# Joint attention block: transposes sorted by width, three value groups of six accumulators, gate rows beside the text scores, gate folded into the last output columns

## The chip, the cores and the metric

The kernel runs on one core of one Trainium2 chip. The core has a matrix engine (TensorE, PE in the profile, with its weight loads as a row of their own, PEld), VectorE (DVE), ScalarE (ACT), GpSimd (POOL) and SyncE (SP), which issues most DMAs. The metric is device time of one execution in microseconds (us). The kernel before takes 124.08 us, median of three runs (123.66 to 124.31).

## The reference

Image tokens (2 batches of 256) and text tokens (2 batches of 32), all of width 1152, are normalised, scaled and shifted by rows computed from a conditioning vector, projected to queries, keys and values with separate weights, attended jointly, projected out with separate weights, gated and added to the input:

```python
hi = _layernorm(x_img) * (1 + sci) + shi      # text: ht, with sct and sht
qkvi = hi @ wqkv_img                          # text: qkvt = ht @ wqkv_txt
q = jnp.concatenate([qt, qi], axis=1)         # k and v likewise: 288 tokens a batch
scores = jnp.einsum('bqd,bkd->bqk', q, k) * D ** (-0.5)
p = _softmax(scores, axis=-1)
a = jnp.einsum('bqk,bkd->bqd', p, v)
out_i = x_img + gai * (ai @ wo_img)
out_t = x_txt + gat * (at @ wo_txt)
```

gai and gat are the third of six slices of silu(c) @ wmod; only the first three slices are used. All is bfloat16 in memory, sums are float32.

## The kernel before, in words

The order of every engine's work is written by hand; a tile framework adds the semaphores. Fourteen weight blocks of 1152 x 1152 (2.6 MB each) are loaded by SyncE's queue into six buffers that are used in turn (`wpool`). PSUM, where matmuls write, is held as seven banks in turn (`ps_mm`) and one more (`ps_sm`).

Up to about 78 us the kernel normalises and projects. Then come the stages that the change touches.

- Scores. `scores_txt` (L456) computes the 32 text queries of both batches, the two batches side by side in tiles of 128 rows by 32 columns. `scores_img(b, qi)` (L448) computes 128 image queries against the batch's 288 keys with 9 matmuls. Each is followed by a softmax: a maximum on VectorE, an exponential with row sum on ScalarE. The text weights are divided by their sum at once (`softmax_txt_norm`); the image rows are divided only at the output. `mod_rows(w_ga_i, 3)` (L344) computes the image gate row for both batches in four tiles of 128 x 32; it goes through a scratch in device memory (L354) and comes back, broadcast to all partitions, as `gb` (L543), both by POOL's queue. The order is: text scores, two image blocks of batch 0, gate rows, two image blocks of batch 1.
- Transposes. `p_transposes(b)` turns the softmax weights with TensorE: for each image block two 128 x 128 pieces (L486, image keys) and two copies of the 32 text keys, at the partitions where text values will lie (L488, 128*32), then the text queries' pieces (L493, 32*128, and L496, 32*32). ScalarE copies the image-key part out of PSUM as `pT` (L499), VectorE the text-key part as `pX` (L501). `v_txt` computes the text values between the two batches' transposes: 1024 columns in two tiles side by side (L525), then the remaining 128 (L528).
- Value stage. `attn_out` makes the attention output transposed, in nine tiles of 128 columns for each batch: `aT`. Groups of two column tiles and two batches, four accumulators, and a last group of two: first the image keys (L510, 128*128, two matmuls each), then the text keys (L516, 32*128, one each; the four of a group lie in four different row strips). The casts to `aT` alternate between VectorE and ScalarE (`evac`, L142 and L144).
- Output. `out_tile(i)` (L578) multiplies 128 image tokens with the output weights, in chunks of 384 columns and nine matmuls; VectorE multiplies a chunk with the inverse row sum and the gate (L581) and adds the input (L583), and SP's queue stores it. The order is image tiles 0 and 1, the text gate rows, image tile 2, the text output (L597, L601, L602, stored by SP and by ScalarE's queue, L605), and image tile 3 in chunks of 384, 384, 256 and 128 with a store for each (L585).

Of the kernel before, what the change touches and what calls it, by code (L numbers as in the profile page):

```python
# [9 lines left out]
ALU = mybir.AluOpType  # L10
# [4 lines left out]
def kernel(  # L15
# [14 lines left out]
    nc = tc.nc  # L30
    bf = mybir.dt.bfloat16
    f32 = mybir.dt.float32
    PSUM = bass.MemoryType.PSUM

    B, NI, D = x_img.shape
    NT = x_txt.shape[1]
    P = 128
    KT = D // P
    NTOK = NI + NT
    NIT = (B * NI) // P  # L40
    TPB = NI // P
    NTT = B * NT
    CH = 384
# [10 lines left out]
    wpool = ctx.enter_context(tc.tile_pool(name="w", bufs=6))  # L54
    act = ctx.enter_context(tc.tile_pool(name="act", bufs=1))
    work = ctx.enter_context(tc.tile_pool(name="work", bufs=2))
    small = ctx.enter_context(tc.tile_pool(name="small", bufs=4))
    ps_mm = ctx.enter_context(tc.tile_pool(name="ps_mm", bufs=7, space=PSUM))
    ps_sm = ctx.enter_context(tc.tile_pool(name="ps_sm", bufs=1, space=PSUM))
# [22 lines left out]
    x_i = act.tile([P, NIT, D], bf)  # L82
# [25 lines left out]
    ident = const.tile([P, P], bf)  # L108
# [186 lines left out]
    v_t = act.tile([P, VW], bf)  # L295
    v_t8 = act.tile([NTT, P], bf)
    pbs = {}
# [13 lines left out]
    ps = ps_mm.tile([P, VW], f32, tag="mm")  # L311
# [24 lines left out]
    NGG = 4  # L336
    gsc = tc.dram_tile([5, B, D], bf, name="mod_scratch")

    def mod_rows(w_blk, si, add_one=False, lhs=None):
        lhs = sT32 if lhs is None else lhs  # L340
        gps = ps_mm.tile([P, VC], f32, tag="mm")
        for kt in range(KT):
            for g in range(NGG):
                nc.tensor.matmul(gps[32 * g:32 * g + 32, :], lhsT=lhs[:, kt, :], rhs=w_blk[:, kt, g * VC:(g + 1) * VC],  # L344
                                 start=(kt == 0), stop=(kt == KT - 1), tile_position=(0, 32 * g))
        g_sb = work.tile([P, VC], bf, tag="garow")
        if add_one:
            nc.vector.tensor_scalar_add(g_sb[:], gps[:], 1.0)
        else:
            evac(g_sb[:], gps[:])  # L350
        if si is None:
            return g_sb
        for b in range(B):
            nc.gpsimd.dma_start(gsc[si, b, :].rearrange("(g j) -> g j", g=NGG), g_sb[b:P:32, :])  # L354
# [89 lines left out]
    def scores_img(b, qi):  # L444
        q0 = qi * P
        sps = ps_mm.tile([P, NTOK], f32, tag="mm")
        for ft in range(KT):
            nc.tensor.matmul(sps[:], lhsT=qkT[:, ft, b, q0:q0 + P], rhs=qkT[:, KT + ft, b, :],  # L448
                             start=(ft == 0), stop=(ft == KT - 1))
        softmax_img(sps, (b, qi))  # L450

    def scores_txt():
        sps = ps_mm.tile([P, NTOK], f32, tag="mm")
        for ft in range(KT):
            for b in range(B):
                nc.tensor.matmul(sps[NT * b:NT * (b + 1), :], lhsT=qkT[:, ft, b, NI:NTOK], rhs=qkT[:, KT + ft, b, :],  # L456
                                 start=(ft == 0), stop=(ft == KT - 1), tile_position=(0, NT * b))
        return sps

    def softmax_txt(sps):  # L460
        q = NTT
        nmx = small.tile([P, 1], f32, tag="nmx")
        nc.vector.reduce_max(nmx[0:q, :], sps[0:q, :], axis=AX.X, negate=True)
        e = work.tile([P, NTOK], f32, tag="e", bufs=1)
        rs = small.tile([P, 1], f32, tag="rst", bufs=1)
        nc.scalar.activation(e[0:q, :], sps[0:q, :], ACT.Exp, bias=nmx[0:q, :], scale=1.0, accum_out=rs[0:q, :])
        return e, rs

    def softmax_txt_norm(e, rs):
        q = NTT  # L470
        nc.vector.reciprocal(rs[0:q, :], rs[0:q, :])
        nc.vector.tensor_scalar_mul(pbs["t"][0:q, :], e[0:q, :], rs[0:q, :])
# [4 lines left out]
    def p_transposes(b):  # L477

        pT_ps = ps_mm.tile([P, 2, NTOK], bf, tag="mm")
        pX_ps = ps_mm.tile([P, NTOK], bf, tag="mm")  # L480
        rows = [32 * (2 * g + b) for g in range(2)]
        for qi in range(TPB):
            qp = qpos[b][qi]
            pb = pbs[(b, qi)]
            for kj in range(2):
                nc.tensor.transpose(pT_ps[:, kj, qp:qp + P], pb[:, kj * P:(kj + 1) * P], ident[:])  # L486
            for r in rows:
                nc.tensor.transpose(pX_ps[r:r + NT, qp:qp + P], pb[:, NI:NTOK], ident[:])  # L488
        qp = qpos[b][2]
        pb = pbs["t"]  # L490
        r0 = NT * b
        for kj in range(2):
            nc.tensor.transpose(pT_ps[:, kj, qp:qp + NT], pb[r0:r0 + NT, kj * P:(kj + 1) * P],  # L493
                                ident[r0:r0 + NT, r0:r0 + NT])
        for r in rows:
            nc.tensor.transpose(pX_ps[r:r + NT, qp:qp + NT], pb[r0:r0 + NT, NI:NTOK], ident[r0:r0 + NT, r0:r0 + NT])  # L496
        pT = work.tile([P, 2, NTOK], bf, tag="pT")
        pX = work.tile([P, NTOK], bf, tag="pX")
        nc.scalar.copy(pT[:], pT_ps[:])  # L499
        for r in rows:  # L500
            nc.vector.tensor_copy(pX[r:r + NT, :], pX_ps[r:r + NT, :])  # L501
        pTs[b] = pT
        pXs[b] = pX

    def attn_out():
        for dts in [(i, NGG + i) for i in range(NGG)] + [(2 * NGG,)]:
            accs = [(dt, b, ps_mm.tile([P, NTOK], f32, tag="mm", name="aps")) for dt in dts for b in range(B)]
            for (dt, b, aps) in accs:
                for kj in range(TPB):
                    nc.tensor.matmul(aps[:], lhsT=v_i[:, b * TPB + kj, dt * P:(dt + 1) * P], rhs=pTs[b][:, kj, :],  # L510
                                     start=(kj == 0), stop=False)
            for (dt, b, aps) in accs:
                g, blk = divmod(dt, NGG)
                r = 32 * (2 * (g % 2) + b)
                lhsT = v_t[r:r + NT, blk * P:(blk + 1) * P] if g < 2 else v_t8[r:r + NT, :]
                nc.tensor.matmul(aps[:], lhsT=lhsT, rhs=pXs[b][r:r + NT, :], start=False, stop=True)  # L516
            for (dt, b, aps) in accs:
                evac(aT[:, dt, b * NTOK:(b + 1) * NTOK], aps[:])

    def v_txt():  # L520
        ps = ps_mm.tile([P, VW], f32, tag="mm")
        ps8 = ps_mm.tile([P, P], f32, tag="mm")
        for kt in range(KT):
            for g in range(2):
                nc.tensor.matmul(ps[64 * g:64 * g + NTT, :], lhsT=hT_t[:, kt, :], rhs=w_v_t[:, kt, g * VW:(g + 1) * VW],  # L525
                                 start=(kt == 0), stop=(kt == KT - 1), tile_position=(0, 64 * g))
        for kt in range(KT):
            nc.tensor.matmul(ps8[0:NTT, :], lhsT=hT_t[:, kt, :], rhs=w_v_t[:, kt, NM:D],  # L528
                             start=(kt == 0), stop=(kt == KT - 1), tile_position=(0, 0))
        nc.vector.tensor_copy(v_t[:], ps[:])  # L530
        nc.scalar.copy(v_t8[:], ps8[0:NTT, :])

    sps_t = scores_txt()
    st_sm = softmax_txt(sps_t)
    scores_img(0, 0)
    softmax_txt_norm(*st_sm)
    scores_img(0, 1)
    mod_rows(w_ga_i, 3)
    scores_img(1, 0)
    scores_img(1, 1)  # L540
    gb = act.tile([P, B, D], bf, tag="Bt")
    for b in range(B):
        nc.gpsimd.dma_start(gb[:, b, :], gsc[3, b, :].partition_broadcast(P))  # L543
    p_transposes(0)
    v_txt()
    p_transposes(1)
    aT = act.tile([P, KT, B * NTOK], bf, tag="Q")
    attn_out()
    for key in sorted(rsum):
# [11 lines left out]
    def txt_gate_spread(g_sb):  # L561
        for r in range(2):
# [2 lines left out]
                             start=True, stop=True)  # L565
            nc.scalar.copy(gbf[:, r, :], bps[:])

    def out_tile(i, chunks, per_chunk):
        b, qi = i // TPB, i % TPB
        t0 = b * NTOK + qpos[b][qi]  # L570
        dst = oi_flat[i * P:(i + 1) * P, :]
        o = work.tile([P, D], bf, tag="o")
        c0 = 0
        for cw in chunks:
            cs = slice(c0, c0 + cw)
            ps = ps_mm.tile([P, CH], f32, tag="mm")
            for dt in range(KT):
                nc.tensor.matmul(ps[:, 0:cw], lhsT=aT[:, dt, t0:t0 + P], rhs=w_o_i[:, dt, cs],  # L578
                                 start=(dt == 0), stop=(dt == KT - 1))
            tmp = work.tile([P, CH], bf, tag="tmp")  # L580
            nc.vector.scalar_tensor_tensor(tmp[:, 0:cw], ps[:, 0:cw], rsum[(b, qi)][:], gb[:, b, cs],  # L581
                                           op0=ALU.mult, op1=ALU.mult)
            nc.vector.tensor_add(o[:, cs], tmp[:, 0:cw], x_i[:, i, cs])  # L583
            if per_chunk:
                nc.sync.dma_start(dst[:, cs], o[:, cs])  # L585
            c0 += cw
        if not per_chunk:
            nc.sync.dma_start(dst, o[:])

    def out_txt():  # L590
# [12 lines left out]
        for g in range(2):  # L603
            eng = nc.sync if g == 0 else nc.scalar
            eng.dma_start(ot_flat.rearrange("t (r g j) -> g t r j", r=2, g=2)[g], of[64 * g:64 * g + NTT, :, :])  # L605

    full = (CH,) * NCH
    out_tile(0, full, False)
    out_tile(1, full, False)
# [35 lines left out]
```

## Time and profile before

| | |
|---|---|
| median of three runs | 124.08 us (123.66 to 124.31) |
| the profiled execution | 123.83 us, span of its instructions 122.0 us |
| TensorE's granted clock | 0.995 |
| scores, from 78.42 us | 6.96 us |
| first transposes to first value matmul, 85.38 to 89.97 | 4.59 us |
| value stage, 89.97 to 96.49 | 6.52 us |
| output, 96.49 to VectorE's last instruction at 119.10 | 22.61 us |
| DMA | 41.63 MB; 409, 401 and 418 GB/s in the scores, transposes and value stage, 234 GB/s in the output up to 113.65 |

Times in the text count from the first instruction of the profiled execution. A line of a timeline gives start, length, engine, line of the kernel, operation, result and operands, the tile of the array (rows*columns) for TensorE, shapes and count; in square brackets the idle time before and what released it. A matmul's end is modelled, so consecutive starts say more than lengths. The chain is followed back from the last instruction to what released each step.

### The profile page before, as it was taken

What the parts mean: (1) busy time and instruction counts of PE and PEld (TensorE: products, weight loads), DVE (VectorE), ACT (ScalarE), POOL (GpSimd) and SP (SyncE); (2) the same over time, 40 slices, a digit from 0 to 9 for tenths busy, and PEclk for the clock granted to TensorE, in tenths of its full rate; (3) what the DMA queues carried; (4) which work ended last, traced back from release to release, by engine and by line L of the source; (5) the groups of instructions that cost most, each with busy time, mean ns of one, the idle gap of its engine ahead of it and who ended that gap; (6) DMA issues with size and microseconds to landing.
All of it is one profiled execution on the core that took longest, in us unless ns stands there. A gap on an engine that the chain in (4) does not pass through costs nothing.

```text
span 122.0 us, 2687 instructions
## 1 busy us (share of the span) xinstructions
PE 113.3 (93%) x1149; PEld 65.4 (54%) x1149; DVE 55.7 (46%) x132; ACT 31.7 (26%) x72; POOL 21.3 (17%) x53
## 2 busy tenths in 40 slices
PE   5865989999999999999999999999999999999970
PEld 1243644546864445445444449967556555667650
DVE  1788642257580222912030621153345766636680
ACT  4554530231690301010031122133424500012000
POOL 4005433520074020304230000003052000000000
PEclk9999999999999999999999999999999999999997
DMA  3999999999999999999999999999999999520231
GB/s 110 288 362 376 377 379 348 346 413 411 405 411 403 407 413 416 411 401 411 408 373 339 410 410 407 410 406 412 405 410 416 381 411 404 218 97 0 102 104 44
DMA packets 22727, 41.63 MB, mean 341 GB/s; under 512 B 1147, under 2 KB 6427, under 8 KB 22715
## 3 DMA queue, kind: packets, MB, share of 16 engines
q1 hardware_dynamic: 21776, 39.74, 86.7%
q0 software_dynamic: 768, 1.64, 3.6%
q8 instruction: 9, 0.15, 0.4%
q10 hardware_dynamic: 171, 0.08, 0.2%
q14 instruction: 3, 0.02, 0.1%
HBM read 40.11 MB, written 1.35 MB: 340 GB/s over the span
## 4 chain that ended last, share of the span: by engine, by line
PE 83%; DMA 6%; SPq 3%; DVE 2%; ACT 2%; issue 1%
PE qkps L388 29%; PE ps L578 13%; PE va L215 9%; DMA w_sc_i<-in_wmod_img_dram 6%; PE gps L344 5%; PE aps L510 4%; PE ps L428 4%; PE sps L448 4%; PE mps L176 3%; PE ps L597 2%; PE ps L525 2%; PE ps L306 2%; SPq L87 2%; PE ps L313 2%; ACT hT_i L169 2%; SPq L92 1%
## 5 line engine op out<-in xcount | busy, mean ns | idle before, releaser
L388 PE MATMUL qkps<-hT_i,t 128*128 128x512 bf16 x162 | 35.7, 379 | 0.0
L388 PEld LDWEIGHTS <-t 128*128 128x128 bf16 x162 | 15.5, 98 | 18.9 <-issue 0.7
L578 PE MATMUL ps<-t,aT 128*128 128x384 bf16 (+2 forms) x117 | 18.1, 314 | 0.0
L215 PE MATMUL va<-w_v_i,hT_i 128*128 128x512 bf16 x63 | 14.7, 379 | 0.1
L578 PEld LDWEIGHTS <-aT 128*128 128x128 bf16 x117 | 10.9, 98 | 6.8 <-issue 0.5
L581 DVE SCALAR_TENSOR_TENSOR tmp<-ps,rs,gb 128x384 bf16<-128x384 f32 (+2 forms) x13 | 7.6, 587 | 6.9 <-PE ps L578 6.9
L354 POOL DMA_DIRECT2D mod_scratch<-g_sb x8 | 4.8, 598 | 34.1 <-DVE g_sb L142 22.3
L215 PEld LDWEIGHTS <-hT_i 128*128 128x128 bf16 x63 | 5.9, 97 | 6.2 <-issue 0.4
L199 POOL TENSOR_SCALAR hT_i<-hT_i,mod_img 128x128 bf16<-128x128 bf16 (+1 forms) x14 | 6.2, 453 | 13.1 <-ACT mod_img L186 5.7
L372 DVE TENSOR_SCALAR qkT<-qkps 128x512 bf16<-128x512 f32 x5 | 3.4, 687 | 9.1 <-PE qkps L388 9.1
L144 ACT CAST qkT<-qkps 128x512 bf16<-128x512 f32 x5 | 2.8, 587 | 16.0 <-PE qkps L388 16.0
L142 DVE CAST qkT<-qkps 128x512 bf16<-128x512 f32 x4 | 2.8, 688 | 8.5 <-PE qkps L388 8.5
L123 PE MATMUL wps<-wz 128*128 128x512 bf16 x15 | 5.3, 501 | 1.2 <-DVE wz L113 1.2
L169 ACT COPY hT_i<-tp 128x640 bf16<-128x640 bf16 (+1 forms) x8 | 4.7, 642 | 5.0 <-PE tp L168 5.0
L150 DVE BATCH_NORM_STATS2 stats<-x_i 128x6 f32<-128x384 bf16 x12 | 5.9, 545 | 0.0
L510 PE MATMUL aps<-pT,v_i 128*128 128x288 bf16 x36 | 5.4, 287 | 0.3 <-ACT pT L499 0.3
L374 ACT ACTIVATE qkT<-qkps 128x512 bf16<-128x512 f32 x4 | 2.3, 596 | 11.4 <-PE qkps L388 11.4
L168 PE MATMUL tp<-ident,xn_i 128*128 128x128 bf16 x36 | 2.7, 220 | 2.7 <-DVE xn_i L159 2.7
L344 PE MATMUL gps<-t,sT 128*32 128x288 bf16 x144 | 5.1, 287 | 0.0
L194 DVE TENSOR_SCALAR hT_i<-hT_i,mod_img 128x256 bf16<-128x256 bf16 x14 | 4.3, 369 | 1.5 <-ACT hT_i L169 1.3
L428 PEld LDWEIGHTS <-t 128*128 128x128 bf16 x162 | 4.9, 98 | 0.2
L142 DVE CAST aT<-aps 128x288 bf16<-128x288 f32 x9 | 3.7, 454 | 2.6 <-PE aps L516 2.6
(111 smaller groups left out, 123.7 us busy)
## 6 DMA issues: line engine op xcount, KB each, us to landing
t<-in_wmod_txt_dram SPq DMA_DIRECT2D x3, 2592.0 KB, 23.4
t<-in_wqkv_txt_dram SPq DMA_DIRECT2D x3, 2592.0 KB, 20.7
t<-in_wmod_img_dram SPq DMA_DIRECT2D x2, 2592.0 KB, 19.1
t<-in_wqkv_img_dram SPq DMA_DIRECT2D x6, 864.0 KB, 16.4
t<-in_wo_img_dram SPq DMA_DIRECT2D x1, 2592.0 KB, 22.5
t<-in_wo_txt_dram SPq DMA_DIRECT2D x1, 2592.0 KB, 24.6
w_sc_i<-in_wmod_img_dram SPq DMA_DIRECT2D x3, 576.0 KB, 7.1
w_v_i<-in_wqkv_img_dram SPq DMA_DIRECT2D x3, 576.0 KB, 7.8
```

Source lines behind the costliest of these rows:

```text
L123: nc.tensor.matmul(ps[:], lhsT=wz[:, 0:P], rhs=wz[:], start=True, stop=True)
L142: nc.vector.tensor_copy(out_ap, in_ap)
L150: nc.vector.bn_stats(stats[0:np_, k, :], x_ap[:, k * CH:(k + 1) * CH])
L169: nc.scalar.copy(hT_i[:, k0:k1, i * P:(i + 1) * P], tp[:, 0:k1 - k0, :])
L199: nc.gpsimd.tensor_scalar(sl, sl, ap, 0.0, op0=ALU.mult, op1=ALU.add)
L215: nc.tensor.matmul(ps[:], lhsT=hT_i[:, kt, i * P:(i + 1) * P], rhs=w_v_i[:, kt, half * VW:(half + 1) * VW], start=(kt == 0), stop=(kt == K ...
L344: nc.tensor.matmul(gps[32 * g:32 * g + 32, :], lhsT=lhs[:, kt, :], rhs=w_blk[:, kt, g * VC:(g + 1) * VC], start=(kt == 0), stop=(kt == KT ...
L388: nc.tensor.matmul(pss[j - j0][:], lhsT=wq[:, kt, j * P:(j + 1) * P], rhs=hT_i[:, kt, :], start=(kt == 0), stop=(kt == KT - 1))
L428: nc.tensor.matmul(ps[:, j - j0, :], lhsT=wq[:, kt, j * P:(j + 1) * P], rhs=hT_t[:, kt, :], start=(kt == 0), stop=(kt == KT - 1))
L510: nc.tensor.matmul(aps[:], lhsT=v_i[:, b * TPB + kj, dt * P:(dt + 1) * P], rhs=pTs[b][:, kj, :], start=(kj == 0), stop=False)
L578: nc.tensor.matmul(ps[:, 0:cw], lhsT=aT[:, dt, t0:t0 + P], rhs=w_o_i[:, dt, cs], start=(dt == 0), stop=(dt == KT - 1))
L581: nc.vector.scalar_tensor_tensor(tmp[:, 0:cw], ps[:, 0:cw], rsum[(b, qi)][:], gb[:, b, cs], op0=ALU.mult, op1=ALU.mult)
```

## The change

Four edits, all from the scores on.

- The two image score blocks of batch 0 come first, then the text scores, directly behind them the gate rows; the text softmax's division follows the gate rows.
- `p_transposes` issues its transposes by tile shape: the four of 128*128, then the text queries' 32*128 and 32*32, then the four of 128*32. `v_txt` is split: the wide part stays between the two batches, the narrow part comes after the second batch's transposes.
- `attn_out` has three groups of three column tiles and two batches: (0, 4, 1), (2, 5, 3), (6, 8, 7). One accumulator of each group uses the single bank of `ps_sm`. Within a group all of batch 0 comes first for the image keys; for the text keys the first two column tiles come first, then the third, whose row strips are those of the first or second. The output matmuls take the column tiles in the order 0 to 6, 8, 7.
- A new function `gate_weights` lets POOL multiply the last 384 columns of the output weights with batch 1's gate, nine products, into a weight buffer `w_og`. The last image tile's chunks of 256 and 128 use it; VectorE then needs one instruction for each of these chunks instead of two. The 256 chunk's store moves from SP's queue to ScalarE's.

```diff
@@ p_transposes @@
+        qt = qpos[b][2]
+        pt = pbs["t"]
+        r0 = NT * b
         for qi in range(TPB):
-            qp = qpos[b][qi]
-            pb = pbs[(b, qi)]
             for kj in range(2):
-                nc.tensor.transpose(pT_ps[:, kj, qp:qp + P], pb[:, kj * P:(kj + 1) * P], ident[:])
-            for r in rows:
-                nc.tensor.transpose(pX_ps[r:r + NT, qp:qp + P], pb[:, NI:NTOK], ident[:])
+                nc.tensor.transpose(pT_ps[:, kj, qpos[b][qi]:qpos[b][qi] + P], pbs[(b, qi)][:, kj * P:(kj + 1) * P],
+                                    ident[:])
...
         for r in rows:
-            nc.tensor.transpose(pX_ps[r:r + NT, qp:qp + NT], pb[r0:r0 + NT, NI:NTOK], ident[r0:r0 + NT, r0:r0 + NT])
+            nc.tensor.transpose(pX_ps[r:r + NT, qt:qt + NT], pt[r0:r0 + NT, NI:NTOK], ident[r0:r0 + NT, r0:r0 + NT])
+        for qi in range(TPB):
+            for r in rows:
+                nc.tensor.transpose(pX_ps[r:r + NT, qpos[b][qi]:qpos[b][qi] + P], pbs[(b, qi)][:, NI:NTOK], ident[:])
@@ attn_out @@
+    def attn_acc(dt, b, own):
+        if own:
+            return (dt, b, ps_sm.tile([P, NTOK], f32, tag="sm", name="aps"))
+        return (dt, b, ps_mm.tile([P, NTOK], f32, tag="mm", name="aps"))
+
     def attn_out():
-        for dts in [(i, NGG + i) for i in range(NGG)] + [(2 * NGG,)]:
-            accs = [(dt, b, ps_mm.tile([P, NTOK], f32, tag="mm", name="aps")) for dt in dts for b in range(B)]
+        for dts, own in (((0, 4, 1), 0), ((2, 5, 3), 1), ((6, 8, 7), 1)):
+            accs = [attn_acc(dt, b, (dt, b) == (dts[0], own)) for b in range(B) for dt in dts]
             for (dt, b, aps) in accs:
                 for kj in range(TPB):
                     nc.tensor.matmul(aps[:], lhsT=v_i[:, b * TPB + kj, dt * P:(dt + 1) * P], rhs=pTs[b][:, kj, :],
                                      start=(kj == 0), stop=False)
+            accs.sort(key=lambda a: (a[0] == dts[2], dts.index(a[0]), a[1]))
@@ order of scores, transposes and text values @@
-    sps_t = scores_txt()
-    st_sm = softmax_txt(sps_t)
     scores_img(0, 0)
+    scores_img(0, 1)
+    st_sm = softmax_txt(scores_txt())
+    mod_rows(w_ga_i, 3)
     softmax_txt_norm(*st_sm)
-    scores_img(0, 1)
-    mod_rows(w_ga_i, 3)
     scores_img(1, 0)
     scores_img(1, 1)
...
     p_transposes(0)
-    v_txt()
+    v_txt_wide()
     p_transposes(1)
+    v_txt_rest()
@@ output @@
+    DTS = (0, 1, 2, 3, 4, 5, 6, 8, 7)
+    NG0 = 2 * CH
+    w_og = wpool.tile([P, KT, D], bf, tag="w", name="w_og")
+
+    def gate_weights():
+        for dt in range(KT):
+            nc.gpsimd.tensor_mul(w_og[:, dt, 0:CH], w_o_i[:, dt, NG0:D], gb[:, B - 1, NG0:D])
...
-            for dt in range(KT):
-                nc.tensor.matmul(ps[:, 0:cw], lhsT=aT[:, dt, t0:t0 + P], rhs=w_o_i[:, dt, cs],
-                                 start=(dt == 0), stop=(dt == KT - 1))
-            tmp = work.tile([P, CH], bf, tag="tmp")
-            nc.vector.scalar_tensor_tensor(tmp[:, 0:cw], ps[:, 0:cw], rsum[(b, qi)][:], gb[:, b, cs],
-                                           op0=ALU.mult, op1=ALU.mult)
-            nc.vector.tensor_add(o[:, cs], tmp[:, 0:cw], x_i[:, i, cs])
+            gated = per_chunk and c0 >= NG0
+            for dt in DTS:
+                rhs = w_og[:, dt, c0 - NG0:c0 - NG0 + cw] if gated else w_o_i[:, dt, cs]
+                nc.tensor.matmul(ps[:, 0:cw], lhsT=aT[:, dt, t0:t0 + P], rhs=rhs,
+                                 start=(dt == DTS[0]), stop=(dt == DTS[-1]))
+            if gated:
+                nc.vector.scalar_tensor_tensor(o[:, cs], ps[:, 0:cw], rsum[(b, qi)][:], x_i[:, i, cs],
+                                               op0=ALU.mult, op1=ALU.add)
+            else:
+                tmp = work.tile([P, CH], bf, tag="tmp")
+                ...
             if per_chunk:
-                nc.sync.dma_start(dst[:, cs], o[:, cs])
+                eng = nc.scalar if c0 == NG0 else nc.sync
+                eng.dma_start(dst[:, cs], o[:, cs])
...
+    gate_weights()
     full = (CH,) * NCH
     out_tile(0, full, False)
```

`v_txt_wide` and `v_txt_rest` are the two loops of `v_txt`, each followed by its own copy out of PSUM (VectorE for the wide part, ScalarE for the narrow one).

More of the change, by code (lines that the diff above doesn't have):

```diff
@@ L481, in p_transposes @@
         rows = [32 * (2 * g + b) for g in range(2)]
+        qt = qpos[b][2]
+        pt = pbs["t"]
+        r0 = NT * b
         for qi in range(TPB):
-            qp = qpos[b][qi]
-            pb = pbs[(b, qi)]
             for kj in range(2):
-                nc.tensor.transpose(pT_ps[:, kj, qp:qp + P], pb[:, kj * P:(kj + 1) * P], ident[:])
-            for r in rows:
[L488 to L491, printed above, removed]
+                nc.tensor.transpose(pT_ps[:, kj, qpos[b][qi]:qpos[b][qi] + P], pbs[(b, qi)][:, kj * P:(kj + 1) * P],
+                                    ident[:])
         for kj in range(2):
-            nc.tensor.transpose(pT_ps[:, kj, qp:qp + NT], pb[r0:r0 + NT, kj * P:(kj + 1) * P],
+            nc.tensor.transpose(pT_ps[:, kj, qt:qt + NT], pt[r0:r0 + NT, kj * P:(kj + 1) * P],
                                 ident[r0:r0 + NT, r0:r0 + NT])
         for r in rows:
-            nc.tensor.transpose(pX_ps[r:r + NT, qp:qp + NT], pb[r0:r0 + NT, NI:NTOK], ident[r0:r0 + NT, r0:r0 + NT])
+            nc.tensor.transpose(pX_ps[r:r + NT, qt:qt + NT], pt[r0:r0 + NT, NI:NTOK], ident[r0:r0 + NT, r0:r0 + NT])
+        for qi in range(TPB):
+            for r in rows:
+                nc.tensor.transpose(pX_ps[r:r + NT, qpos[b][qi]:qpos[b][qi] + P], pbs[(b, qi)][:, NI:NTOK], ident[:])
         pT = work.tile([P, 2, NTOK], bf, tag="pT")
@@ L518, in attn_out, with v_txt_wide @@
                 evac(aT[:, dt, b * NTOK:(b + 1) * NTOK], aps[:])
-    def v_txt():
+    def v_txt_wide():
         ps = ps_mm.tile([P, VW], f32, tag="mm")
-        ps8 = ps_mm.tile([P, P], f32, tag="mm")
         for kt in range(KT):
@@ L526, in v_txt, with v_txt_rest @@
                                  start=(kt == 0), stop=(kt == KT - 1), tile_position=(0, 64 * g))
+        nc.vector.tensor_copy(v_t[:], ps[:])
+    def v_txt_rest():
+        ps8 = ps_mm.tile([P, P], f32, tag="mm")
         for kt in range(KT):
@@ L529, in v_txt @@
                              start=(kt == 0), stop=(kt == KT - 1), tile_position=(0, 0))
-        nc.vector.tensor_copy(v_t[:], ps[:])
         nc.scalar.copy(v_t8[:], ps8[0:NTT, :])
-    sps_t = scores_txt()
-    st_sm = softmax_txt(sps_t)
     scores_img(0, 0)
+    scores_img(0, 1)
+    st_sm = softmax_txt(scores_txt())
+    mod_rows(w_ga_i, 3)
     softmax_txt_norm(*st_sm)
-    scores_img(0, 1)
-    mod_rows(w_ga_i, 3)
     scores_img(1, 0)
@@ L576, in out_tile @@
             ps = ps_mm.tile([P, CH], f32, tag="mm")
-            for dt in range(KT):
-                nc.tensor.matmul(ps[:, 0:cw], lhsT=aT[:, dt, t0:t0 + P], rhs=w_o_i[:, dt, cs],
-                                 start=(dt == 0), stop=(dt == KT - 1))
-            tmp = work.tile([P, CH], bf, tag="tmp")
-            nc.vector.scalar_tensor_tensor(tmp[:, 0:cw], ps[:, 0:cw], rsum[(b, qi)][:], gb[:, b, cs],
-                                           op0=ALU.mult, op1=ALU.mult)
-            nc.vector.tensor_add(o[:, cs], tmp[:, 0:cw], x_i[:, i, cs])
+            gated = per_chunk and c0 >= NG0
[8 more added lines that the diff above has]
+                tmp = work.tile([P, CH], bf, tag="tmp")
+                nc.vector.scalar_tensor_tensor(tmp[:, 0:cw], ps[:, 0:cw], rsum[(b, qi)][:], gb[:, b, cs],
+                                               op0=ALU.mult, op1=ALU.mult)
+                nc.vector.tensor_add(o[:, cs], tmp[:, 0:cw], x_i[:, i, cs])
             if per_chunk:
-                nc.sync.dma_start(dst[:, cs], o[:, cs])
+                eng = nc.scalar if c0 == NG0 else nc.sync
+                eng.dma_start(dst[:, cs], o[:, cs])
             c0 += cw
```

## The prediction

> **What bounds the kernel now.** I read the page's busy shares and chain first, then the chain in order of time from 60 us on, then TensorE's timeline of the attention stretch, last the end of the run on VectorE.
>
> ```profile
> PE 113.3 (93%) x1149; PEld 65.4 (54%) x1149; DVE 55.7 (46%) x132; ACT 31.7 (26%) x72; POOL 21.3 (17%) x53
> PE 83%; DMA 6%; SPq 3%; DVE 2%; ACT 2%; issue 1%
> ```
>
> TensorE is 93% busy and carries 83% of the chain, so a microsecond taken from its sequence is a microsecond of the end, as long as the weights are there. They are: in the table of issues and landings, counted from the issue, the text value weights land at 61.30 + 23.3 = 84.6 (first used at 86.39), the image output weights at 68.89 + 22.5 = 91.4 (96.49), the text gate weights at 75.32 + 24.5 = 99.8 (105.37), the text output weights at 81.59 + 24.6 = 106.2 (111.33). The smallest cover is 1.8 us, at the text values.
>
> TensorE's timeline, scores to transposes of the first batch; columns are start, length, line, tile rows*columns, shape, count:
>
> ```profile
> 78.42 1.28 PE L456 MATMUL sps<-qkT 128*32 128x288 bf16 x18
> 79.63 2.38 PE L448 MATMUL sps<-qkT 128*128 128x288 bf16 x18
> 81.94 1.29 PE L344 MATMUL gps<-t,sT 128*32 128x288 bf16 x36
> 83.16 2.38 PE L448 MATMUL sps<-qkT 128*128 128x288 bf16 x18
> 85.38 0.28 PE L486 MATMUL pT_ps<-ident,pb 128*128 128x128 bf16 x2
> 85.58 0.23 PE L488 MATMUL pX_ps<-ident,pb 128*32 128x128 bf16 x2
> 85.75 0.28 PE L486 MATMUL pT_ps<-ident,pb 128*128 128x128 bf16 x2
> 85.96 0.23 PE L488 MATMUL pX_ps<-ident,pb 128*32 128x128 bf16 x2
> 86.13 0.21 PE L493 MATMUL pT_ps<-ident,pb_tt 32*128 32x32 bf16 x2
> 86.27 0.19 PE L496 MATMUL pX_ps<-ident,pb_tt 32*32 32x32 bf16 x2
> ```
>
> Ends are modelled, so I go by starts. The last 18 score matmuls take 83.16 to 85.38 = 2.22, or 0.123 each, and the tile stays 128*128 behind them. The same 18, followed by another tile shape, take 79.63 to 81.94 = 2.31: 0.09 more. The 36 gate matmuls, four at a time, should take 9 x 0.123 = 1.11 and take 1.22: 0.11 more. So **a change of tile shape costs about 0.105 us** on TensorE.
>
> The chain in order of time, value stage (start, length, piece):
>
> ```profile
> 89.96 0.65 ACT pT L499
> 90.61 0.04 issue
> 90.65 0.90 PE aps L510 x6
> 91.54 0.23 PE aps L516 x4
> 91.78 1.09 PE aps L510 x8
> 92.86 0.23 PE aps L516 x4
> ```
>
> Each group of four accumulators is 8 image matmuls in 1.09 (8 x 0.123 + one change) and four concurrent text matmuls in 0.23 (one 0.123 and one change). Ahead of the second accumulator TensorE waits for ScalarE's copy of the second batch's transposed weights: two matmuls from 89.97 would be done at 90.22, and it goes on at 90.65, 0.43 lost.
>
> The end, on VectorE:
>
> ```profile
> 117.44 0.36 DVE L583 TENSOR_TENSOR o<-tmp,x_i 128x384 bf16<-128x384 bf16 x1
> 117.77 0.48 DVE L581 SCALAR_TENSOR_TENSOR tmp<-ps,rs,gb 128x256 bf16<-128x256 f32 x1
> 118.29 0.29 DVE L583 TENSOR_TENSOR o<-tmp,x_i 128x256 bf16<-128x256 bf16 x1
> 118.50 0.34 DVE L581 SCALAR_TENSOR_TENSOR tmp<-ps,rs,gb 128x128 bf16<-128x128 f32 x1
> 118.88 0.22 DVE L583 TENSOR_TENSOR o<-tmp,x_i 128x128 bf16<-128x128 bf16 x1
> ```
>
> TensorE's last matmuls start at 118.0; VectorE, with no idle time in these lines, ends at 119.10. Here VectorE sets the end, then the last store (1.4 to land) and the close at 122.0.
>
> **The change part by part.** *Scores.* The gate rows (128*32) now stand directly behind the text scores (128*32), and both first-batch score blocks ahead of them. Changes of shape from the first score to the transposes fall from three to two: -0.11. The change ahead of the text scores goes too, but the first score still waits for VectorE's last cast (77.74 + 0.56 = 78.30, against a start at 78.42): 0 to -0.1, taken as 0. The text softmax is needed at the transposes, 3 us later; the gate rows' scratch writes and the broadcast behind them move by those 0.1.
>
> *Transposes.* The steps of one batch by starts are 0.20, 0.17, 0.21, 0.17, 0.14, 0.12 = 1.01. Sorted, four 128*128 stand together (0.20 + 2 x 0.055 = 0.31; 0.055 is a 128-column matmul, from the nine of L528: 0.60 less one change, over 9), then 0.14 and 0.12, then four 128*32, two at a time (0.17 + 0.055 = 0.225): 0.795. Two batches: -0.43. The narrow text-value block moves behind the second batch's transposes and gets its own change: +0.10. Together -0.33.
>
> *Value stage.* Before, 89.97 to 96.49 = 6.52: 36 x 0.123 + 5 x 0.123 + 10 changes x 0.105 + 0.43 wait = 6.52, so the account closes. After: 36 x 0.123 = 4.43; text matmuls four and then two, because the third column tile shares its rows with the first: 6 x 0.123 = 0.74; six changes 0.63; sum 5.80. The wait goes: three accumulators of the first batch (0.74) and the narrow text block (0.60) now cover the copy of 0.65. What is late next is the banks. Casts as before (after the text matmuls start, VectorE has done one at 0.81, two at 1.18, three at 1.65; ScalarE 0.78, 1.08, 1.55) free them, ScalarE those of the first batch, VectorE those of the second. Group two starts 0.35 after that point, takes VectorE's first bank at 0.84 and ScalarE's third at 1.58: waits of 0 to 0.1; group three has more room. I take 0.1: 5.90, -0.62. Bounds: -0.72 with no wait and 0 if the second text wave costs another 0.1 and the banks 0.2 in each of the two later groups.
>
> The row for one row group is the image stretch: eight 128-row matmuls run 0.136 apart although each needs a new weight load of 0.098, so loads hide there, and I cost the second text wave at 0.123. The Trainium skill, "TensorE: Matmul & The Clock Gate", section "The mechanism" of Part 3, says that a weight load overlaps running matmuls only where its row group differs; by it each second wave (rows of the first) would show its load of 0.09, +0.27 in three groups, and the gain would be 1.28 where the sum below has 1.55.
>
> *Gate folded into the output columns.* Nine new POOL products of 128x384 with two inputs. No such row exists; one-input POOL rows are 409 ns at 128x128 and 512 at 128x256, 0.8 ns per element, so 0.61 at 384 as the low end; twice that plus 0.2 (POOL rows grow from 371 to 575 ns beside VectorE) is 1.43 as the high end; I take 1.0. They start when the second gate broadcast lands, 90.5 + 5.8 = 96.3, and end between 101.8 and 109.2. The first is wanted by the 256-column block of the last tile: 113.65 + 2 x 1.46 = 116.57, now near 115.5. Cost nothing, cover 6 to 13 us; behind them POOL's queue has no work. The price beside them is VectorE's: L194 takes 274 to 511 ns beside POOL. Output chunks use 0.62 + 0.36 of 1.46 us; two such growths fill a chunk's slack, and with seven banks nothing reaches TensorE. The Trainium skill, "GPSIMD Engine Reference", Key points, names VectorE instructions with two SBUF inputs as contending with GpSimd, which here is the residual addition.
>
> *End.* The last two residual additions go. The 256 block still starts at 117.77 (VectorE's own order) and ends at 118.25; the 128 block follows at 118.27 and ends at 118.61 instead of 119.10: -0.49. The 256 block's store moves from SP to ScalarE's queue, where nothing stands behind it; SP then has the 128 block next. A pair of equal stores landed in 2.4 on ScalarE's queue and 2.1 on SP's: the 256 store, 0.35 earlier than the last, would at 1.5 + 0.3 land level with it. Bounds -0.2 to -0.55.
>
> Sum: -0.11 - 0.33 - 0.62 - 0.49 = -1.55. The profiled execution is 123.83, so 122.28; it lies 0.25 under the median of 124.08, which would give 122.53. I say 122.4.
>
> **Rivals.** *Banks:* six accumulators leave only two spare banks, and group two waits for evacuations. For it: the margins above are under 0.1. Against: in the trace every cast has the same length within 12 ns. Another 0.4 per later group plus slow second waves is +1.0: 123.3.
>
> *Width is not the cause:* the 0.105 belongs to each stretch's first wait, not to its shape. Then only the copy wait (0.43), the end (0.49) and the extra text waves (-0.37) remain: about 123.3. Against it: L448 to L486, a new stretch with a new wait and the same shape, has no such gap.
>
> *End not gained:* ScalarE's store lands late and closes the run: 122.8.
>
> *Slower:* the POOL products take over (115.5 - 96.3) / 9 = 2.1 us each. TensorE then waits in the last tile; from 2.3 us the gain is gone (1.55 / 9 more), at 2.8 the end is 6.3 - 1.55 = 4.7 later, about 128.5. Against: the highest bound is 1.43.
>
> **How the numbers follow.** Forecast 0.56, banks 0.16, width 0.08, end 0.10, POOL 0.06, and 0.04 for something not seen, mostly later. A difference under 0.5% (0.6 us) can't be told from none. Faster by more: forecast, end, most of width and half of banks, 0.80. Within: 0.11. Slower: 0.09. Low end: the best of every bound (-0.21, -0.43, -0.72, -0.55 = -1.9) and 0.2 for spread, 121.7; high end: the banks' and width's case, 123.5.
>
> **What would show it.** Right: TensorE's starts give three value groups of about 1.93, sorted transposes of 0.8, no wait for the pT copy, the narrow text block between; nine POOL products ended before 110; VectorE's last instruction about 0.5 after the last matmul block rather than 1.1. Wrong: PE idle before L515 released by DVE or ACT, second text waves 0.2 apart, a Pool wait at the 256-column block, or a store on ScalarE's queue that lands last.

## The result, and the profile after

The changed kernel takes 121.89 us (median; 121.44 to 122.18) where the kernel before takes 123.87 beside it: a ratio of 0.9825, with a 95% interval of 0.9804 to 0.9847. That is 1.98 us less. The prediction was 122.4, from a sum of 1.55 us.

The changed kernel's page shows nearly the same busy time on TensorE in a shorter span, and the new POOL products as a group (line, engine, operation, operands, count | busy, mean ns | idle before):

```profile
PE 113.1 (94%) x1149; PEld 65.2 (54%) x1149; DVE 56.3 (47%) x130; ACT 31.5 (26%) x72; POOL 29.9 (25%) x62
L582 POOL TENSOR_TENSOR w_og<-t,gb 128x384 bf16<-128x384 bf16 x9 | 8.7, 1000 | 5.3 <-DMA t<-in_wmod_txt_dram 5.3
```

TensorE's timeline of the changed kernel, in the columns of the one before (start, length, line, tile rows*columns, shape, count):

```profile
78.82 2.37 PE L448 MATMUL sps<-qkT 128*128 128x288 bf16 x18
...
85.65 0.39 PE L487 MATMUL pT_ps<-ident,pb 128*128 128x128 bf16 x4
85.97 0.21 PE L490 MATMUL pT_ps<-ident,pb_tt 32*128 32x32 bf16 x2
86.11 0.19 PE L493 MATMUL pX_ps<-ident,pb_tt 32*32 32x32 bf16 x2
86.22 0.29 PE L496 MATMUL pX_ps<-ident,pb 128*32 128x128 bf16 x4
86.44 2.13 PE L530 MATMUL ps<-t,hT_t 128*64 128x512 bf16 x18
...
89.31 0.69 PE L537 MATMUL ps<-t,hT_t 128*64 128x128 bf16 x9
89.94 1.64 PE L515 MATMUL aps<-pT,v_i 128*128 128x288 bf16 x12
91.51 0.42 PE L522 MATMUL aps<-pX,v_t 32*128 32x288 bf16 x6
91.86 1.67 PE L515 MATMUL aps<-pT,v_i 128*128 128x288 bf16 x12
93.46 0.42 PE L522 MATMUL aps<-pX,v_t 32*128 32x288 bf16 x6
...
95.74 1.47 PE L596 MATMUL ps<-t,aT 128*128 128x384 bf16 x8
```

The sorted transposes of a batch go from 85.65 to 86.44, 0.79 us; a value group takes 91.86 to the next group's start at 93.81, 1.95; no line carries idle time for the copy of pT. The six text matmuls of a group take 91.51 to 91.86 = 0.35, which is two waves of 0.123 and one change of shape: the second wave's weight loads do not show.

The end of the changed kernel, on VectorE and ScalarE's queue:

```profile
116.03 0.62 DVE L603 SCALAR_TENSOR_TENSOR tmp<-ps,rs,gb 128x384 bf16<-128x384 f32 x1 [0.45 <-PE ps L596]
116.69 0.36 DVE L605 TENSOR_TENSOR o<-tmp,x_i 128x384 bf16<-128x384 bf16 x1
117.02 0.85 DVE L599 SCALAR_TENSOR_TENSOR o<-ps,rs,x_i 128x256 bf16<-128x256 f32 x2
117.53 0.39 ACTq L608 DMA_DIRECT2D out_dram<-o  x1
```

VectorE ends at 117.87. From there to the end of the span are 2.45 us (to 120.32), where the kernel before needs 2.86 (119.10 to 121.96). Nothing in the change was meant to touch that stretch, which I call the close. The ends of the span are read to 0.01 us from the traces; the pages round them to 0.1, and the closes named in the expectations below (2.9, 2.43) come from rounded spans and are off by up to 0.05.

The stages of all profiled executions, by TensorE's starts (us). "First" is from the first text key or query matmul (L428) to the first score, "tail" from the last image tile's first matmul to VectorE's last instruction.

| kernel | first | scores | transposes and text values | value stage | output to last tile | tail | close |
|---|---|---|---|---|---|---|---|
| before | 4.82 | 6.96 | 4.59 | 6.52 | 17.16 | 5.45 | 2.86 |
| after | 4.75 | 6.83 | 4.29 | 5.80 | 17.16 | 4.97 | 2.45 |
| end only | 4.82 | 6.95 | 4.60 | 6.52 | 17.16 | 4.97 | 2.46 |
| all but the end | 4.75 | 6.83 | 4.29 | 5.79 | 17.16 | 5.45 | 2.85 |
| POOL memsets | 4.82 | 6.96 | 4.59 | 6.52 | 17.16 | 5.46 | 2.45 |
| value groups only | 4.82 | 6.95 | 4.60 | 5.80 | 17.16 | 5.44 | 2.86 |
| order only | 4.75 | 6.83 | 4.28 | 6.11 | 17.16 | 5.46 | 2.86 |
| more changes of shape | 4.75 | 8.53 | 4.29 | 5.80 | 17.16 | 4.97 | 2.46 |
| wide POOL products | 4.75 | 6.82 | 4.29 | 5.80 | 17.37 | 10.65 | 2.56 |
| 256 store on SP | 4.75 | 6.82 | 4.30 | 5.79 | 17.16 | 4.97 | 2.59 |
| joint transposes | 4.75 | 6.92 | 3.75 | 5.80 | 17.16 | 4.97 | 2.47 |
| joint, rows together | 4.75 | 6.92 | 3.74 | 5.81 | 17.16 | 4.97 | 2.46 |
| after once more | 4.75 | 6.83 | 4.29 | 5.79 | 17.17 | 4.97 | 2.46 |

A stage repeats to 0.01 or 0.02 from one execution to the next. The starting point does not: L428 begins between 73.5 and 74.2 in these executions, at 73.6 in the one before and 74.1 in the one after, because the first weights that TensorE waits for land at 12.0 and at 12.5, in a part that no edit touches. That is why the two spans differ by 1.6 while the stages differ by 2.1. Below, small effects are read from the stages and the sum from the medians.

### The profile page after: what moved, and what is told of

The parts are those of the page before. It is cut to its first block, busy times and chain, and to the rows that moved or that the text cites. A ratio compares the mean times of both kernels' runs of the same rounds, so it can differ in the third digit from the quotient of the medians.

```text
span 120.3 us, 2697 instructions
## 1 busy us (share of the span) xinstructions
PE 113.1 (94%) x1149; PEld 65.2 (54%) x1149; DVE 56.3 (47%) x130; ACT 31.5 (26%) x72; POOL 29.9 (25%) x62
## 4 chain that ended last, share of the span: by engine, by line
PE 83%; DMA 6%; SPq 3%; DVE 2%; ACT 2%; issue 1%
PE qkps L388 29%; PE ps L596 14%; PE va L215 9%; DMA w_sc_i<-in_wmod_img_dram 6%; PE gps L344 5%; PE aps L515 4%; PE ps L428 4%; PE sps L448 4%; PE mps L176 3%; PE ps L620 2%; PE ps L530 2%; PE ps L306 2%; PE ps L313 2%; SPq L87 2%; ACT hT_i L169 2%; SPq L92 1%
## 5 line engine op out<-in xcount | busy, mean ns | idle before, releaser
L596 PE MATMUL ps<-t,aT 128*128 128x384 bf16 x99 | 16.6, 326 | 0.0
L582 POOL TENSOR_TENSOR w_og<-t,gb 128x384 bf16<-128x384 bf16 x9 | 8.7, 1000 | 5.3 <-DMA t<-in_wmod_txt_dram 5.3
L603 DVE SCALAR_TENSOR_TENSOR tmp<-ps,rs,gb 128x384 bf16<-128x384 f32 x11 | 6.8, 617 | 5.1 <-PE ps L596 5.0
L123 PE MATMUL wps<-wz 128*128 128x512 bf16 x15 | 6.0, 557 | 1.2 <-DVE wz L113 1.2
L605 DVE TENSOR_TENSOR o<-tmp,x_i 128x384 bf16<-128x384 bf16 x11 | 5.2, 475 | 0.4
L428 PEld LDWEIGHTS <-t 128*128 128x128 bf16 x162 | 4.9, 98 | 0.2
```

The costliest lines, as they stand in the source:

```text
L123: nc.tensor.matmul(ps[:], lhsT=wz[:, 0:P], rhs=wz[:], start=True, stop=True)
L428: nc.tensor.matmul(ps[:, j - j0, :], lhsT=wq[:, kt, j * P:(j + 1) * P], rhs=hT_t[:, kt, :], start=(kt == 0), stop=(kt == KT - 1))
L582: nc.gpsimd.tensor_mul(w_og[:, dt, 0:CH], w_o_i[:, dt, NG0:D], gb[:, B - 1, NG0:D])
```

## The experiments

**The end alone.** The kernel before, with `gate_weights`, the gated last chunks and the 256 store on ScalarE's queue.

```diff
+    gate_weights()
     full = (CH,) * NCH
 ...
+                eng = nc.scalar if c0 == NG0 else nc.sync
+                eng.dma_start(dst[:, cs], o[:, cs])
```

> The kernel before with the folded gate and the 256 store on ScalarE's queue alone. Theory: VectorE's last instruction comes 0.48 us earlier against the start of the last image tile (4.97 instead of 5.45), and the close from there to the end of the span falls from 2.9 to about 2.45, because POOL has more instructions behind it and no longer sits in the closing barrier: -0.95 us in all. Rival: the shorter close came from the other edits or from chance, then -0.5. Nine POOL products of about 1.0 us end near 107; residual additions beside them grow from 0.36 to about 0.8 with no wait on TensorE.

Measured: 123.19 against 123.89, ratio 0.9929 (0.9903 to 0.9954), -0.70 us. The tail falls by 0.48 and the close by 0.40. The median gives less than the 0.9 of the two stages; its interval, -0.57 to -1.20 us, holds 0.9 and leaves the rival's 0.5 out by little, so the stages decide: the shorter close comes with this part of the change.

**All but the end.** The changed kernel with the old end.

```diff
-    gate_weights()
 ...
-            gated = per_chunk and c0 >= NG0
+                nc.vector.tensor_add(o[:, cs], tmp[:, 0:cw], x_i[:, i, cs])
```

> The changed kernel with the old end (no POOL products, separate residual additions, all stores of the last tile on SP). Theory: stages scores 6.83, transposes 4.29, value stage 5.80, last tile to VectorE's last 5.45, close 2.9: -1.2 us against before. Rival for the close: 2.45, then -1.65.

Measured: 122.48 against 123.89, ratio 0.9878 (0.9843 to 0.9912), -1.41 us. Every stage is where it was expected, and the close is the long one, 2.85. So the first three stages make their gain without the end, and the close does not come from them.

**Twelve memsets on POOL.** The end changes three things at once that could shorten the close: POOL's instructions, VectorE's, and the queue of a store. This kernel changes only the first.

```diff
+    pad = small.tile([P, 12], f32, bufs=1)
+    for i in range(12):
+        nc.gpsimd.memset(pad[:, i:i + 1], 0.0)
+
     def txt_gate():
```

> The kernel before with twelve one-column memsets on POOL behind its last DMA, nothing else. Theory that the length of POOL's instruction stream sets the close: the stages are unchanged, the close falls from 2.9 to about 2.45, -0.45 us. Rival that the close hangs on the stores or on VectorE's end: 0.

Measured: 123.43 against 123.89, ratio 0.9974 (0.9947 to 1.0). The median alone is at the edge of what can be told; the stage is plain, 2.45 against 2.86. POOL's queue at the closing line, in the kernel before (count: shortest/median/longest ns, first to last start; the first line from a window that holds only the first two closing semaphore instructions):

```profile
L640 POOLq EVENT_SEMAPHORE  x2: 17/17/17, 120.8 to 121.3; - x2
L640 POOLq EVENT_SEMAPHORE  x4: 17/17/17, 120.8 to 121.9; - x4
L640 POOLq DRAIN  x2: 46/94/141, 121.3 to 121.7; - x2
```

and the same in the kernel with the memsets:

```profile
L644 POOLq EVENT_SEMAPHORE  x2: 17/17/17, 120.9 to 121.0; - x2
L644 POOLq EVENT_SEMAPHORE  x4: 17/17/17, 120.9 to 121.5; - x4
L644 POOLq DRAIN  x2: 46/72/98, 121.1 to 121.4; - x2
```

POOL's first closing semaphore instruction comes 1.71 and 1.70 us after VectorE's end, so up to there nothing differs. The second comes, read to 0.01 us from the traces, 0.44 us behind the first in the kernel before and 0.08 with the memsets: that is 0.36 of the 0.41. Most of the rest is POOL's drain behind it, 141 ns against 98. The same two steps, 0.44 and 0.08, separate all profiles with a close of 2.85 to 2.86 from all with 2.45 to 2.59.

What goes with it is the place of the last instruction fetch on queue q14. I take this queue for POOL's: its last fetch moves when nothing but POOL's instructions are added. The DMA queues of the kernel before, 121.9 to 122 us (packets, MB, share of the engines):

```profile
q14 instruction: 1, 0.01, 36.2%
```

and of the kernel with the memsets, 95 to 96 us:

```profile
q14 instruction: 1, 0.01, 1.9%
```

The two go together in all thirteen profiles: the fetch falls in the last 0.02 us of the span in the kernel before, "all but the end", "value groups only" and "order only", which have the long close, and at 94 to 97 in the others. But in the kernel before it starts at 121.95, 0.7 us after POOL has gone on at 121.26, so as recorded it can't be what POOL waited for. That adding instructions to POOL's stream shortens the close is shown by this run; what holds POOL between the two instructions stays open.

**The value groups alone.**

```diff
-        for dts in [(i, NGG + i) for i in range(NGG)] + [(2 * NGG,)]:
-            accs = [(dt, b, ps_mm.tile([P, NTOK], f32, tag="mm", name="aps")) for dt in dts for b in range(B)]
+        for dts, own in (((0, 4, 1), 0), ((2, 5, 3), 1), ((6, 8, 7), 1)):
+            accs = [attn_acc(dt, b, (dt, b) == (dts[0], own)) for b in range(B) for dt in dts]
```

> The kernel before with the three groups of six accumulators alone; transposes and text values as before. Theory: four changes of tile shape (0.42) and the wait for the pT copy (0.43) go, one more text wave per group is half made up by fewer groups (+0.12): value stage 5.80 instead of 6.52, -0.72 us, the second text wave 0.12 and not 0.2. Rival that the narrow text block is needed to cover the pT copy: 0.1 to 0.2 less gained.

Measured: 123.26 against 123.89, ratio 0.9945 (0.9922 to 0.9968), -0.63 us; the value stage is 5.80, just as in the changed kernel. Its chain in order of time (start, length, piece):

```profile
90.67 1.58 PE aps L515 x12
92.25 0.35 PE aps L522 x6
92.60 1.60 PE aps L515 x12
```

Putting batch 0 first is enough to cover the copy of pT; the narrow text block is not needed for it. Twelve matmuls and a change are 1.58, so a wait on banks can be no more than the 0.02 between 1.60 and 1.58.

**The order alone.** Scores, transposes and text values as in the changed kernel, groups and end as before.

```diff
-    p_transposes(0)
-    v_txt()
-    p_transposes(1)
+    p_transposes(0)
+    v_txt_wide()
+    p_transposes(1)
+    v_txt_rest()
```

> The new order of scores, transposes and text values alone, with the old groups of four and the old end. Theory: scores 6.83 and transposes 4.29 as in the changed kernel; the value stage 6.09, since the wait of 0.43 for the pT copy is covered by the narrow text block and ten changes remain; end and close as before. Sum -0.13 - 0.30 - 0.43 and 0 to -0.1 at the first score: -0.9. Rival that the groups are needed for the wait to go: -0.5.

Measured in one execution: 123.42 beside 124.34. The value stage is 6.11, so the wait goes here as well, covered by the narrow text block. The wait can be removed by either edit, but only once: the two value-stage gains (0.41 here, 0.72 with the groups alone) do not add. The chain:

```profile
90.13 1.09 PE aps L510 x8
91.22 0.23 PE aps L516 x4
```

**More changes of shape.** A test of the price that carries most of the sum, against the rival that the gaps belong to the first wait of a stretch.

```diff
-    scores_img(0, 1)
-    st_sm = softmax_txt(scores_txt())
+    for ft in range(KT):
+        nc.tensor.matmul(sps01[:], lhsT=qkT[:, ft, 0, P:2 * P], rhs=qkT[:, KT + ft, 0, :], ...)
+        for b in range(B):
+            nc.tensor.matmul(spst[NT * b:NT * (b + 1), :], lhsT=qkT[:, ft, b, NI:NTOK], ...)
```

> The changed kernel with the second image score block (9 matmuls of 128*128) and the text scores (9 pairs of 128*32) issued in turn, one and a pair, instead of one after the other: 17 changes of tile shape where there was one, no new wait, the same matmuls. Theory that a change of shape costs 0.105 us on TensorE: 16 more are +1.7 us on the stretch from the first score to the transposes (6.83 becomes 8.5). Rival that the gaps belong to the first wait of a stretch: 6.8 to 6.9.

Measured: the scores take 8.53, 1.70 more than in the changed kernel, 0.106 for each of the 16. The chain of this kernel:

```profile
80.09 0.23 PE spst L548 x2
80.32 0.23 PE sps L545
80.55 0.23 PE spst L548 x2
```

One matmul, or a pair beside each other, takes 0.23 where it takes 0.123 in a stretch of one shape. There is no wait in these steps. The rival falls.

**Wide POOL products.** POOL multiplies three times the columns; the result of the extra ones is not used.

```diff
-            nc.gpsimd.tensor_mul(w_og[:, dt, 0:CH], w_o_i[:, dt, NG0:D], gb[:, B - 1, NG0:D])
+            nc.gpsimd.tensor_mul(w_og[:, dt, :], w_o_i[:, dt, :], gb[:, B - 1, :])
```

> The changed kernel with POOL multiplying all 1152 columns by the gate where the last 384 are used: products three times as long. At 2.6 to 2.8 us each nine of them end near 122, so TensorE waits for POOL in the 256-column block, about 5.5 us later in all: the place and the price of the slower rival. If the products overlap better than that (2.1 us or less each), nothing is lost. Either way the first-two image tiles' residual additions stay long until POOL is done, without a wait on TensorE before the 256-column block.

Measured: 128.0 beside 124.34 in one execution; span 126.2, 5.9 more than the changed kernel. The size is near the expected 5.5, but only about half of it comes in the expected way. The products' group:

```profile
L582 POOL TENSOR_TENSOR w_og<-t,gb 128x1152 bf16<-128x1152 bf16 x9 | 21.9, 2464 | 5.2 <-DMA gb<-mod_scratch 5.2
```

and the timeline of VectorE and TensorE beside them:

```profile
112.36 0.60 DVE L603 SCALAR_TENSOR_TENSOR tmp<-ps,rs,gb 128x384 bf16<-128x384 f32 x1
113.00 1.88 DVE L605 TENSOR_TENSOR o<-tmp,x_i 128x384 bf16<-128x384 bf16 x1
...
115.44 1.88 DVE L605 TENSOR_TENSOR o<-tmp,x_i 128x384 bf16<-128x384 bf16 x1
115.46 1.62 PE L596 MATMUL ps<-t,aT 128*128 128x384 bf16 x9 [0.82 <-DVE tmp L603]
...
119.59 0.88 PE L596 MATMUL ps<-w_og,aT 128*128 128x256 bf16 x11 [1.74 <-POOL w_og L582]
```

VectorE's scale and gate (one input in PSUM) keeps its 0.60. Its residual addition, with both inputs in SBUF, takes 1.88 instead of 0.36: together one chunk every 2.44, the step from product to product. The addition gets through once per product. So VectorE falls behind from the first chunk, TensorE runs out of banks (0.82), and only then waits for POOL itself (1.74). TensorE's last matmuls end 3.0 later than in the changed kernel (119.59 + 0.88 against 115.83 + 1.65), VectorE 5.8 later: the other 2.8 is work that VectorE still has to catch up with.

**The 256 store on SP's queue.**

```diff
-                eng = nc.scalar if c0 == NG0 else nc.sync
-                eng.dma_start(dst[:, cs], o[:, cs])
+                nc.sync.dma_start(dst[:, cs], o[:, cs])
```

> The changed kernel with the 256 store of the last tile back on SP's queue. The 128 store issues behind it on SP: the 256 result is ready 0.5 before the 128 result and an issue takes 0.33, so nothing waits: span against VectorE's last within 0.1 of the changed kernel's 2.43. Rival that the move to ScalarE's queue gave the shorter close: 2.9.

Measured in one execution: a close of 2.59, 0.13 more than the changed kernel's 2.45 and just outside the 0.1. SP's queue in this kernel, one issue and the next:

```profile
117.63 0.35 SPq L607 DMA_DIRECT2D out_dram<-o  x1
118.08 0.39 SPq L607 DMA_DIRECT2D out_dram<-o  x1
```

The first issue ends at 117.98, just when the last data are there, but the last store is issued only at 118.08, 0.10 after, and its issue takes 0.39. In the changed kernel it is issued at 117.90, 0.03 after its data, and takes 0.33. Together that is the 0.13. The rest of the shorter close stays without the move to ScalarE's queue, so the rival falls.

**Joint transposes.** If a change of shape costs 0.105, the two batches' transposes can share their changes.

```diff
-    p_transposes(0)
-    v_txt_wide()
-    p_transposes(1)
-    v_txt_rest()
+    v_txt_wide()
+    p_transposes_both()      # 8 of 128*128, 4 of 32*128, 4 of 32*32, 8 of 128*32
+    v_txt_rest()
```

> The changed kernel with the wide text values ahead of both batches' transposes, the transposes of both batches sorted together by tile shape, the narrow text values behind them. Ten changes of shape between the last score and the first value matmul become seven: 4.29 becomes 3.97, -0.32 us against the changed kernel, -2.3 against before. ScalarE's two copies (0.65 each) start when the 32*128 pieces are done, some 0.75 into the transposes; the narrow block covers the first. Rival: the text value weights, which land near 84.3, or the copy of the first batch, come late and TensorE waits 0.2 to 0.5: no gain over the changed kernel.

Measured: 121.19 against 123.83, ratio 0.9784 (0.9761 to 0.9806); the changed kernel in the same comparison takes 121.78. TensorE's timeline:

```profile
85.25 2.13 PE L535 MATMUL ps<-t,hT_t 128*64 128x512 bf16 x18
87.32 0.62 PE L488 MATMUL pT_ps<-ident,pb 128*128 128x128 bf16 x8
87.87 0.22 PE L492 MATMUL pT_ps<-ident,pb_tt 32*128 32x32 bf16 x4
88.02 0.20 PE L497 MATMUL pX_ps<-ident,pb_tt 32*32 32x32 bf16 x4
88.14 0.30 PE L502 MATMUL pX_ps<-ident,pb 128*32 128x128 bf16 x8
88.37 0.69 PE L542 MATMUL ps<-t,hT_t 128*64 128x128 bf16 x9
89.00 1.65 PE L520 MATMUL aps<-pT,v_i 128*128 128x288 bf16 x12
```

From the first score to the first value matmul it takes 10.67 where the changed kernel takes 11.12, 0.45 less and more than the 0.32 of the three changes: the four 32*128 pieces take 0.15, where two took 0.14, and eight 128*32 take 0.23, where four took 0.22. The two batches' pieces lie in different strips of the array. No wait appears.

**Rows together.** The joint kernel with the text shift rows ahead of the scale rows.

```diff
-    qk_img(w_q_i, 0, hooks={5: v_shift, 6: txt_rows_shift})
+    qk_img(w_q_i, 0, hooks={5: v_shift})
+    txt_rows_shift()
     txt_rows_scale()
```

> The same, and the text shift rows (128*32) moved from between two query projections to directly ahead of the text scale rows (128*32): two changes of shape fewer, -0.21 us against the run beside it. POOL's scratch writes of the shift rows come about 7 us later and the broadcasts behind them about 1.1 later; the text modulation on VectorE ends near 70 instead of 69, ahead of the text transposes at 71.3. Rival: it ends behind them and TensorE waits, 0 or a loss.

Measured: 121.13, ratio 0.9781 (0.9756 to 0.9806). The two row blocks take 2.32 in one stretch where they took 1.22 twice, and VectorE's text modulation ends at 69.9, ahead of the transposes at 71.1, so the mechanism is there. The traces show the gain: from the first image projection to the first text projection TensorE needs 37.87 (35.58 to 73.45) where the joint kernel needs 38.09 (35.49 to 73.58), 0.22 less, and no later stage is longer by more than 0.01. The medians differ by 0.06 and can't tell it from the joint kernel.

**The changed kernel once more.**

> The changed kernel itself once more, on the same chip as the two before: -2.0 us against before, close 2.43. It gives the ratio of the other two to it.

Measured: 121.78 against 123.83, ratio 0.9832 (0.9805 to 0.9858), and the same stages.

## Why the prediction was right

- *A change of tile shape costs 0.105 us.* Right: 0.106 when sixteen were added.
- *Scores, -0.11.* Measured -0.13, and -0.07 ahead of the first score, where 0 was taken out of a range of 0 to -0.1. The first score starts 0.05 after VectorE's cast ends (78.21 + 0.56 = 78.77), where it started 0.12 after it before, so the cast was not what set it before.
- *Transposes and text values, -0.33.* Measured -0.30; 0.79 for a sorted batch against 0.795; the narrow block's move cost 0.14 and not 0.10.
- *Value stage, -0.62.* Measured -0.72, the bound without bank waits. The banks rival falls: its margins of under 0.1 held. The second text wave cost 0.123. The Trainium skill's rule on weight loads that was weighed ("TensorE: Matmul & The Clock Gate", "The mechanism" of Part 3) would have made a text block of six 0.44; it is 0.35, so here the measurement decides against costing it that way. The 0.136 that the prediction reads between image matmuls is eight matmuls with one change of shape in 1.09; without the change it is 0.123.
- *The width rival* was summed wrongly: it counts 0.37 for the extra text waves, but by the prediction's own account five waves become six, which is 0.12, so it stood near 123.0 and not 123.3. The run with more changes rules it out all the same.
- *POOL products, 1.0 us each and covered.* Measured 1.0 on average. They started at 97.8 and not at 96.3, because the second gate broadcast landed at 97.65, 6.9 us after its issue where 5.8 had been taken (the bracket below names another transfer), and were done at 106.5, about 9 us ahead of their use. What VectorE pays beside them was mis-sized: I gave both of its instructions 0.24; the first grew by nothing, the addition by up to 0.48. It stayed hidden.

The changed kernel's POOL and VectorE, from the timeline:

```profile
97.78 8.72 POOL L582 TENSOR_TENSOR w_og<-t,gb 128x384 bf16<-128x384 bf16 x9 [5.26 <-DMA t<-in_wmod_txt_dram]
98.06 0.84 DVE L605 TENSOR_TENSOR o<-tmp,x_i 128x384 bf16<-128x384 bf16 x1
...
99.52 0.36 DVE L605 TENSOR_TENSOR o<-tmp,x_i 128x384 bf16<-128x384 bf16 x1
```

The Trainium skill, "GPSIMD Engine Reference", Key points, names this pair, GpSimd and a VectorE instruction with two SBUF inputs, among those that contend. The trace agrees, and tells how much: up to the rest of the running product. Here and beside the wide products, each slowed addition ends 0.21 to 0.22 us after the product that ran beside it.
- *End, -0.49.* Measured -0.48 to VectorE's last instruction, as worked out. The store on ScalarE's queue did not land late (1.6 against 1.5 for SP's last).
- *The close was taken as fixed.* This is the step that failed: the prediction carried "the close at 122.0" along as a constant, and it shrank by 0.40. Without it the stages sum to 0.07 + 0.13 + 0.30 + 0.72 + 0.48 = 1.70, against 1.55 forecast; with it 2.10. The medians say 1.98 and, once more, 2.05. So the mechanism that was forecast carries about four fifths of the gain, and the rest came unforeseen, in the favourable direction by luck.
- *The slower rival* had the right place, and its turning point was too late. It counted when POOL is done, 2.1 us per product. With 2.46 it would have given 9 x 0.36 = 3.2 us; 5.9 were measured, because VectorE's addition advances once per product and its backlog outlasts POOL. The 3.2 is close to what TensorE lost (3.0); the other 2.8 is VectorE's.

## What to carry to other kernels

Count the changes of tile shape in TensorE's order, not only its matmuls: at 0.105 us each, a pair of small transposes between two stretches costs more in changes than in work, and sorting across batches shortens it further than sorting within one. A product on POOL is free only while VectorE's two-input SBUF work beside it has room for about one product per addition, so price the neighbour and not just the finish. And the stretch after the last result is a stage too: look at what each queue does there before treating it as a constant.

## What the runs showed that was not expected

- Twelve small POOL instructions, 0.12 us each and of no use, shorten the run's close from 2.86 to 2.45 us. In the kernels with the long close POOL's first two closing semaphore instructions start 0.44 us apart, in the others 0.08. The last instruction fetch falls at the very end of the run in the first and at 94 to 97 us in the others, but it comes after the wait, so the cause stays open.
- A VectorE addition with two SBUF inputs took 0.36 us alone and 1.88 beside products of 2.46 us, while a VectorE instruction with one input in PSUM kept 0.60 to 0.62.
- Four 32*128 transposes of two batches took 0.15 us, two of one batch 0.14.
- Of two stores issued close together on SP's queue the second was issued 0.45 us after the first and 0.10 after its data were there; the two issues took 0.35 and 0.39 us, where issues that stand apart took 0.33.
